# A 16-head masked attention feeding two expert layers on one Trainium2 core: a bank evacuation and four weight-load issues moved along ScalarE's queue

## The chip, the cores and the metric

The kernel runs on one core of a Trainium2 chip. The metric is device time in microseconds (us) of one launch, the median of several runs. The kernel before takes 790.23 us (median of 3 runs, 789.36 to 791.34).

## The reference, cut to what matters

Three layers follow each other. The change lies in the first; the weights that it loads earlier belong to the second.

```python
# attention: B=2, H=8, S=768, D=64 -> 16 heads, 16 clusters per head
q_assign = argmax(normalised q . normalised centroids); k_assign likewise
scores = where(q_assign == k_assign, q @ k.T / sqrt(D), -1e9)
attn = exp(scores - max) ; attn = attn / (sum(attn) + 1e-9)
x = attn @ v                                   # heads side by side: 1536 x 512
# layer 2
h = x @ w_in ; g = s * relu(h)**2 + b ; x = g @ w_out      # d_ff = 2048, float64 weights
# layer 3: each of the 1536 tokens goes to one of 8 experts
out[token] = gate * (relu(x @ w1[e]) @ w2[e])
```

## The kernel before, in words

**Attention is a written-out order.** `attention` (L94) gives every piece of work a time on one line: head `j` owns the 12 slots from `12*j`, and a piece with offset `t` in the table `TIMES` (L31) stands at `12*j + t`. All pieces are sorted by this number (L375) and `Order.pin` (L59) keeps each engine's instructions in that order. So a number in the table sets only the order in each engine's queue; when an instruction runs is decided by its waits. Below, "frame k" is the stretch of head `k`'s twelve slots, and pieces of heads before and after fall into it.

In a frame TensorE (PE) does, slot by slot, one product `M` for a later head (L223; VectorE reduces it to a row maximum, L224) and one pair of products `S` for this head (L247, L248; ScalarE turns it into `pt` with Exp, L249). `S` has two tile names for the two halves of a row of keys, `s0` and `s1`, one PSUM bank each, so the pair of slot 5 writes the bank that the Exp of slot 3 reads. `V` (L264) multiplies `pt` with the values into the single bank `pv`: six groups per head, done two by two at slots 5.45, 9.45 and 1.45 of the next frame. `pv_out` (L272) is two ScalarE instructions that read this bank, `vm` (L276) and `xu` (L277); the next head's first `V`, at slot 5.45, overwrites it. `trans` (L157) turns `k` and `q` of a head three frames ahead: three PE transposes into the single bank `t` (L162) and one ScalarE copy out of it (`kb` or `qb`, L168). The two for `k` stand at slots 11.4 and 0.4, the two for `q` at 2.4 and 3.4; of each two the second waits for the copy of the first. `mrow` (L232, slot 8.5) writes the row maxima of the next head as one row of `qa`: a ScalarE copy `mrs` (L237) and a DMA on SyncE's queue (L238, `qa<-mrs`). The next head's first `S`, at slot 0 of the next frame, reads that row.

**Weights of layer 2.** `conv_steps` (L416) turns one 128-row piece of the float64 weights to float32 in nine steps, and the last step calls `load_f64` (L523) for the piece three further on: two DMAs of 512 KB, `w_in` (L525) and `w_out` (L526), into the pool `raw`. For the pieces 0 to 3 these are issued from ScalarE's queue, at the time `36*f + 16 + CONV[8]`. With `CONV[8]` = 31.2 this is slot 11.2 of frames 3, 6, 9 and 12. Three first loads (`FETCH`, slot 5.3 of frames 0, 1 and 2) are issued from the same queue.

```python
37   CONV = (3.2, 5.2, 7.2, 11.2, 15.2, 19.2, 23.2, 27.2, 31.2)
373  for i, f in enumerate((pv_out, sums, norm_a, norm_b, norm_c)):
374      at(o + ENDS.get(j, T["norm"])[i], f, j)
407  for n, t in enumerate(CONV):
408      out.append((36 * f + 16 + t if f < NWA - 1 else 176.2 + n, ...
276  nc.scalar.activation(out=vm, in_=pp[:, HS:HS + 1], func=AF.Copy, scale=GUARD / S)
277  nc.scalar.activation(out=xu, in_=pp[:, 0:HS], func=AF.Identity, bias=vm[:, 0:1])
```

Of the kernel before, what the change touches and what calls it, by code (L numbers as in the profile page):

```python
# [28 lines left out]
MASK = float(2 ** 33)  # L29
GUARD = 1e-9  # L30
TIMES = dict(load=-49, loadv=-18, split=(-42, -40), trans=(-36.6, -35.6, -33.6, -32.6), sims=-30.53, simv=(-26.5, -26.5, -26.5, -22.52, -22.52, -22.51),  # L31
             M=-17.4, mneg=-5.7, mrow=-3.5, V=(5.45, 5.45, 9.45, 9.45, 13.45, 13.45), presum=3.0, norm=(14.5, 25.47, 29.5, 29.5, 29.5))
ENDS = {14: (14.5, 21.47, 22.4, 23.4, 24.4), 15: (14.5, 14.6, 14.7, 14.8, 14.9)}
WARM = -26
HEAT = ((-41, 7), (-30.5, 6), (-22, 6))
SETUP, FETCH = 6.3, (5.3, 17.3, 29.3)
CONV = (3.2, 5.2, 7.2, 11.2, 15.2, 19.2, 23.2, 27.2, 31.2)
F, DM, TC = 2048, 512, 512
NF, KD, NTT = F // P, DM // P, TC // P
E, F2 = 8, 1024  # L40
# [53 lines left out]
def attention(ax, tc, cst, q, k, v, cen, xt, hooks, embed):  # L94
# [124 lines left out]

    def M(j, r, c):  # L220
        i = j % NSET
        pp = ps([P, HS], "M", f"M{c}" if j else ("M0", "M1", "s0", "s1", "s2")[(2 * r + c) % 5])
        nc.tensor.matmul(pp, qa[i][0:80, r * P:(r + 1) * P], ka[i][0:80, c * HS:(c + 1) * HS])  # L223
        nc.vector.tensor_reduce(out=mxt[j % 2][:, r, c:c + 1], in_=pp, axis=AX.X, op=ALU.max)  # L224
# [112 lines left out]
    def at(t, f, *a):  # L337
        ops.append((t, len(ops), f, a))
# [9 lines left out]
    for j in range(NH):  # L348
# [12 lines left out]
        for r in range(NR):  # L361
            for c in range(2):
                at(o + T["M"] + 2 * r + c, M, j, r, c)
                if j == 0:
                    at(o + T["M"] + 2 * r + c, cst.heat, 2, "pv")
        at(o + T["mneg"], mneg, j)
# [14 lines left out]
class Moe:  # L381
# [11 lines left out]
    def hooks(self, ms, mb):  # L393
# [12 lines left out]
        for f in range(NWA):  # L406
            for n, t in enumerate(CONV):
                out.append((36 * f + 16 + t if f < NWA - 1 else 176.2 + n, lambda f=f: next(self.steps(f), None)))
# [51 lines left out]
    def ps(self, shape, name, tag):  # L460
        return self.cst.ps(shape, name, dict(a="pv", b="sm", y0="t", y1="s0", y2="s1", y3="s2").get(tag, tag))
# [124 lines left out]
    def moe1(self, xt):  # L586
# [4 lines left out]
        for c in range(self.chunks):  # L591
# [4 lines left out]
            def up(f):  # L596
# [4 lines left out]
                if final:  # L601
                    self.load_expert(f + 1)
                    if f in PRE0:
                        z = PRE0.index(f)
                        with self.after(*tail):
                            self.pre0[z] = self.half(self.wraw[0, z], 0, nc.gpsimd, False)
                hp = self.ps([P, TC], "hp", f"M{f % 2}")
                self.up_mm(hp, *wu, lambda k: x[k // 2][:, k % 2], lambda k: x[2 + k // 2][:, k % 2])
# [446 lines left out]
    def block(self, y, args, w, pre, hooks, wd=None, g0=None):  # L1055
# [7 lines left out]
        def up(f):  # L1063
            with ExitStack() as behind:
# [5 lines left out]
                if f not in wd:  # L1070
                    wd[f] = self.half(w[f], 1, nc.vector)
            hp = self.ps([P, T], "hp", f"M{f % 2}")
            if xl is None:
# [121 lines left out]
```

## Time and profile before

| | |
|---|---|
| median of 3 runs | 790.23 us (789.36 to 791.34) |
| the profiled execution's own time | 785.38 us |
| its span, first to last instruction | 783.5 us, mean granted TensorE clock 0.987 |
| PE busy over the span | 747.7 us (95%) |
| DVE (VectorE), ACT (ScalarE), POOL (GpSimd) busy | 518.4, 423.3, 352.1 us |

The profile is of one execution. Times in rows are us from the span's start. An engine's name with a q is its instruction queue (ACTq, SPq): those rows are DMA issues, during which the queue takes nothing else. PEld is the weight load of a product. A row's last part in brackets is the time that the engine sat idle before it, and what the profile takes for the end of that wait. Products overlap on PE, so the step from one start to the next says what one costs, not its own duration.

### The profile page before, as it was taken

Reading aid. Unit: us, or ns where it says so; the run is one execution under the profiler, and the core shown is the slowest. Engines: PE = TensorE matmul, PEld = TensorE weight load, DVE = VectorE, ACT = ScalarE, POOL = GpSimd, SP = SyncE. Lnnn points to the kernel's source line nnn. Section 1 sums busy time; section 2 is a strip of 40 time slices with the busy share of each in tenths; the row PEclk is TensorE's granted clock in tenths of the full one; section 3 lists DMA queues with packets and bytes.
Section 4 is the critical chain, followed back from the end, with each engine's and each line's share of the span. In section 5 each row is a group of like instructions: output and inputs, shape, how many; then the busy total and the mean of one; then the engine's idle time right before and its main releaser. Section 6 shows DMA issues by size and latency. Waiting matters only on the chain. (4 is left out here: it accounts for less than half of the span.)

```text
span 783.5 us, 12256 instructions
## 1 busy us (share of the span) xinstructions
PE 747.7 (95%) x4193; PEld 564.0 (72%) x4193; DVE 518.4 (66%) x1100; ACT 423.3 (54%) x843; POOL 352.1 (45%) x282
## 2 busy tenths in 40 slices
PE   7799999999999899999999999999999999999993
PEld 3465555565555468888787887877879998988983
DVE  5768989797997889984354442557567365755750
ACT  5266555655554576555445564454557365755650
POOL 3166776676685565445333544467132302230001
PEclk9899999999999999999999999999999999999997
DMA  5145443434322225511000042265235555865600
GB/s 154 42 129 176 107 124 81 140 87 135 79 64 80 69 61 171 161 55 54 1 1 1 1 161 82 81 215 167 80 117 177 184 192 179 250 215 195 220 17 24
DMA packets 75678, 88.72 MB, mean 113 GB/s; under 512 B 7526, under 2 KB 58630, under 8 KB 75345
## 3 DMA queue, kind: packets, MB, share of 16 engines
q1 hardware_dynamic: 66688, 66.52, 28.1%
q0 software_dynamic: 4208, 13.90, 5.5%
q10 hardware_dynamic: 4704, 7.34, 2.8%
q8 instruction: 40, 0.66, 0.3%
q14 instruction: 38, 0.30, 0.1%
HBM read 70.57 MB, written 7.34 MB: 99 GB/s over the span
## 5 line engine op out<-in xcount | busy, mean ns | idle before, releaser
L534 POOL TENSOR_TENSOR wl<-w,wh 128x512 fp32r<-128x512 f32 x96 | 123.0, 1306 | 128.8 <-ACT wh L532 126.1
L249 ACT ACTIVATE pt<-S 128x384 f32<-128x384 f32 x192 | 91.8, 489 | 101.1 <-PE S L248 98.8
L224 DVE TENSOR_REDUCE mx<-M 128x1 f32<-128x384 f32 x192 | 101.9, 552 | 37.1 <-PE M L223 34.6
L260 POOL TENSOR_TENSOR acc<-acc,pt 128x768 f32<-128x768 f32 x61 | 106.0, 1737 | 5.7 <-ACT pt L249 3.3
L555 PE MATMUL hp<-x,wh 128*128 128x512 f32 x384 | 105.1, 395 | 0.3 <-ACT wh L532 0.3
L555 PE MATMUL hp<-x,spare 128*128 128x256 f32 x732 | 96.0, 284 | 2.0 <-PEq L987 1.7
L555 PEld LDWEIGHTS hp<-x,spare 128*128 128x128 f32 x732 | 92.6, 190 | 6.9 <-issue 4.1
L563 PE MATMUL y<-wd,gg 128*128 128x512 f32 x360 | 93.2, 394 | 0.0
L611 DVE SCALAR_TENSOR_TENSOR hp<-hp,sb,t 128x512 f32<-128x512 f32 x48 | 36.4, 758 | 74.6 <-ACT t L610 74.6
L223 PE MATMUL M<-ka,qa 80*128 80x384 f32 x192 | 79.0, 412 | 4.2 <-DVE mx L224 3.1
L555 PEld LDWEIGHTS hp<-x,wh 128*128 128x128 f32 x384 | 70.6, 188 | 15.1 <-ACT wh L532 0.9
L563 PE MATMUL y<-wh,gh 128*128 128x512 f32 x192 | 74.9, 390 | 0.0
L563 PE MATMUL y<-wl,gh 128*128 128x512 f32 x192 | 74.7, 389 | 0.0
L247 PE MATMUL S<-qa,ka 97*128 97x384 f32 x192 | 71.0, 370 | 2.1 <-ACT pt L249 1.4
L268 PE MATMUL pv<-pt,vn 128*64 128x385 f32 x384 | 72.8, 500 | 0.0
L548 DVE TENSOR_TENSOR wd<-w,wd 128x512 fp32r<-128x512 f32 x64 | 43.3, 686 | 44.1 <-ACT wd L547 43.3
L563 PEld LDWEIGHTS y<-wd,gg 128*128 128x128 f32 x360 | 63.8, 189 | 9.9
L1036 POOL DMA_INDIRECT row<-rows,idx x24 | 27.9, 1163 | 88.0 <-PE tp L1048 49.1
L248 PE MATMUL S<-qb,kb 128*128 128x384 f32 x192 | 65.5, 341 | 0.0
L610 ACT ACTIVATE t<-hp 128x512 f32<-128x512 f32 x48 | 28.7, 598 | 67.6 <-PE hp L555 67.5
L223 PEld LDWEIGHTS M<-ka,qa 80*128 80x128 f32 x192 | 36.9, 192 | 38.2 <-DVE su L296 8.1
L532 ACT ACTIVATE wh<-w 128x1024 fp32r<-128x1024 f32 x48 | 50.4, 1055 | 17.7 <-PE y L563 12.9
(275 smaller groups left out, 1352.2 us busy)
## 6 DMA issues: line engine op xcount, KB each, us to landing
w<-in_moe_w_dram SPq DMA_DIRECT2D x128, 256.0 KB
raw<-in_moe_w_in_dram SPq DMA_DIRECT2D x9, 512.0 KB
raw<-in_moe_w_out_dram SPq DMA_DIRECT2D x9, 512.0 KB
raw<-in_moe_w_in_dram ACTq DMA_DIRECT2D x7, 512.0 KB
raw<-in_moe_w_out_dram ACTq DMA_DIRECT2D x7, 512.0 KB
qn<-in_q_dram SPq DMA_DIRECT2D x16, 192.0 KB
kn<-in_k_dram SPq DMA_DIRECT2D x16, 192.0 KB
vn<-in_v_dram SPq DMA_DIRECT2D x16, 192.0 KB
```

Source lines behind the costliest of these rows:

```text
L223: nc.tensor.matmul(pp, qa[i][0:80, r * P:(r + 1) * P], ka[i][0:80, c * HS:(c + 1) * HS])
L224: nc.vector.tensor_reduce(out=mxt[j % 2][:, r, c:c + 1], in_=pp, axis=AX.X, op=ALU.max)
L247: nc.tensor.matmul(pp, ka[i][0:97, t * P:(t + 1) * P], qa[i][0:97, w], start=True, stop=False)
L248: nc.tensor.matmul(pp, kb[i][:, t * P:(t + 1) * P], qb[i][:, w], start=False, stop=True)
L249: exps.setdefault((j, t), []).append(nc.scalar.activation(out=p[:, c, 0:HS], in_=pp, func=AF.Exp, scale=0.125).ins)
L260: eng.tensor_tensor(out=acc[j][-1], in0=acc[j][-1], in1=p[:, :, 0:HS], op=ALU.add)
L268: together(tc, [lambda c=c: nc.tensor.matmul(pv_t[j][c * 64:c * 64 + 64, :], io_t["v", j][:, t, :], p[:, c, :], start=t == 0, stop=t == NR ...
L532: nc.scalar.activation(out=wh, in_=w, func=AF.Copy)
L534: eng.tensor_tensor(out=wl[:, a], in0=w[:, a], in1=wh[:, a].bitcast(F32), op=ALU.subtract)
L548: eng.tensor_tensor(out=t[:, 1], in0=w[:, a], in1=t[:, 0].bitcast(F32), op=ALU.subtract)
L555: self.nc.tensor.matmul(hp, a[:, k * P:(k + 1) * P], b(k), start=n == 0, stop=n == 3 * KD - 1)
L563: self.nc.tensor.matmul(y[i], (gl if n == 2 else gh)[:, s], wl if n == 1 else wh, start=first and n == 0, stop=last and n == 2)
```

## The change

Two numbers of the tables change. `pv_out` of heads 0 to 13 moves from slot 14.5 to 15.45 of its head, that is from slot 2.5 to 3.45 of the next frame. The issue of the four pairs of weight loads moves from slot 11.2 to 9.48 of frames 3, 6, 9 and 12.

```diff
 TIMES = dict(load=-49, ...
-             M=-17.4, ..., presum=3.0, norm=(14.5, 25.47, 29.5, 29.5, 29.5))
+             M=-17.4, ..., presum=3.0, norm=(15.45, 25.47, 29.5, 29.5, 29.5))
 ENDS = {14: (14.5, 21.47, 22.4, 23.4, 24.4), 15: (14.5, 14.6, 14.7, 14.8, 14.9)}
...
-CONV = (3.2, 5.2, 7.2, 11.2, 15.2, 19.2, 23.2, 27.2, 31.2)
+CONV = (3.2, 5.2, 7.2, 11.2, 15.2, 19.2, 23.2, 27.2, 29.48)
```

Only ScalarE's queue is reordered. In frame 10, around slot 3, the queue reads as follows (`qb` are the copies out of the query transposes, `pt` the Exps):

```order
 L249 ACTIVATE pt_129<-S 128x384
 L168 ACTIVATE qb_117<-tp 128x384
-L276 ACTIVATE vm<-pv 128x1
-L277 ACTIVATE xu<-pv,vm 128x384
 L249 ACTIVATE pt_129<-S 128x384
 L168 ACTIVATE qb_117<-tp 128x384
+L276 ACTIVATE vm<-pv 128x1
+L277 ACTIVATE xu<-pv,vm 128x384
 L249 ACTIVATE pt_130<-S 128x384 x2
```

The evacuation of `pv` goes behind one Exp (slot 3) and the second query copy. Frames 1 to 12 look like this; in frames 13 and 14, where no head is left to transpose, it goes behind the Exp alone.

On PE nothing moves, but the waits do. In frame 10 at slot 5.45 the program before has:

```order
L247 MATMUL S<-qa_110,ka_114 128x384 [waits Activation_49]
L248 MATMUL S<-qb_118,kb_122 128x384
L268 MATMUL pv<-pt_128,vn 64x385 x2
L268 MATMUL pv<-pt_129,vn 64x385 x2
L178 MATMUL si<-qb_117,cc 32x384 [waits Activation_49]
```

and the changed one:

```order
L247 MATMUL S<-qa_110,ka_114 128x384 [waits Activation_49]
L248 MATMUL S<-qb_118,kb_122 128x384
L268 MATMUL pv<-pt_128,vn 64x385 [waits Activation_49]
L268 MATMUL pv<-pt_128,vn 64x385
L268 MATMUL pv<-pt_129,vn 64x385 x2
```

The first `V` product of the head now has a wait for ScalarE of its own: for `xu`.

In frame 9, around the weight loads, ScalarE's queue reads:

```order
 L237 ACTIVATE mrs<-mr 6x128
 L249 ACTIVATE pt_126<-S 128x384
-L249 ACTIVATE pt_127<-S 128x384 x2
 L525 DMA raw<-in_moe_w_in_dram 128x4x256
 L526 DMA raw<-in_moe_w_out_dram 128x1024
+L249 ACTIVATE pt_127<-S 128x384 x2
 L168 ACTIVATE kb_121<-tp 128x384
```

The two issues go ahead of two Exps, and no longer stand right before the copy `kb`. They now follow the copy `mrs` with one Exp between.

## Rows read from the trace of the kernel before

**Rows 1.** Busy time by engine, 60 to 260 us (PE, PEld, DVE, ACT, POOL; clock, DMA).

```profile
60.00:260.00 200.00, 193.33 (x1088) 116.33 (x1085) 170.99 (x357) 113.53 (x276) 141.31 (x90) 1.00 0.37 105
```

**Rows 2.** Timeline, frame 10, ACT (start, duration, engine, line, operation).

```profile
194.35 0.49 ACT L168 ACTIVATE qb<-tp 128x384 fp32r<-128x384 f32 x1
...
194.93 0.58 ACT L277 ACTIVATE xu<-pv,vm 128x384 f32<-128x384 f32 x1
```

**Rows 3.** Timeline, frame 10, PE.

```profile
194.89 0.45 PE L162 MATMUL tp<-identr,qs 128*128 128x128 f32 x3 [0.21 <-ACT vm L276]
...
195.95 0.44 PE L247 MATMUL S<-qa,ka 97*128 97x384 f32 x1
...
196.50 0.54 PE L268 MATMUL pv<-pt,vn 128*64 128x385 f32 x2
```

**Rows 4.** Timeline, frame 13, PE.

```profile
239.27 0.34 PE L248 MATMUL S<-qb,kb 128*128 128x384 f32 x1
...
240.18 0.34 PE L223 MATMUL M<-ka,qa 80*128 80x384 f32 x1
240.78 0.45 PE L247 MATMUL S<-qa,ka 97*128 97x384 f32 x1 [0.25 <-ACT pt L249]
...
241.33 0.54 PE L268 MATMUL pv<-pt,vn 128*64 128x385 f32 x2
```

**Rows 5.** Timeline, end of frame 9 and start of 10, PE.

```profile
188.71 0.45 PE L223 MATMUL M<-ka,qa 80*128 80x384 f32 x1
188.99 0.34 PE L247 MATMUL S<-qa,ka 97*128 97x384 f32 x1
...
190.00 0.45 PE L162 MATMUL tp<-identr,ks 128*128 128x128 f32 x3 [0.48 <-ACT kb L168]
...
190.98 0.54 PE L268 MATMUL pv<-pt,vn 128*64 128x385 f32 x2
```

**Rows 6.** Timeline, end of frame 8 (no load issued there), PE.

```profile
173.55 0.45 PE L223 MATMUL M<-ka,qa 80*128 80x384 f32 x1
...
175.12 0.54 PE L268 MATMUL pv<-pt,vn 128*64 128x385 f32 x2
```

**Rows 7.** Timeline, end of frame 9, ACT and its queue.

```profile
186.20 0.46 ACT L249 ACTIVATE pt<-S 128x384 f32<-128x384 f32 x1
187.93 0.97 ACT L249 ACTIVATE pt<-S 128x384 f32<-128x384 f32 x2 [1.27 <-PE S L248]
188.47 0.39 ACTq L525 DMA_DIRECT2D raw<-in_moe_w_in_dram  x1
```

**Rows 8.** Timeline, issues of the row of maxima: frame 9, frame 14.

```profile
186.32 0.77 SPq L238 DMA_DIRECT2D qa<-mrs  x1
...
259.22 0.73 SPq L238 DMA_DIRECT2D qa<-mrs  x1
```

**Rows 9.** Timeline, start of frame 15, PE.

```profile
261.13 0.41 PE L247 MATMUL S<-qa,ka 97*128 97x384 f32 x1 [0.43 <-DMA qa<-mrs]
```

**Rows 10.** Timeline, a transfer on SP's queue with no weight load near it (frame 9).

```profile
180.76 0.53 SPq L170 DMA_DIRECT2D qa<-qb  x1
```

**Rows 11.** DMA queues, 181.90 to 183.10 us (packets, MB, share of 16 engines; q1 is SP's).

```profile
q1 hardware_dynamic: 80, 0.20, 74.3%
```

**Rows 12.** Timeline, ACT's and SP's queue, frame 0.

```profile
42.71 0.43 ACTq L525 DMA_DIRECT2D raw<-in_moe_w_in_dram  x1
...
43.06 0.54 SPq L170 DMA_DIRECT2D qa<-qb  x1
```

**Rows 13.** DMA queues, 44.21 to 45.80 us (q10, ACT's, is the only one listed).

```profile
q10 hardware_dynamic: 353, 0.36, 82.0%
```

**Rows 14.** Timeline, SP's and ACT's queue, frame 1.

```profile
57.87 0.58 SPq L123 DMA_DIRECT2D vn<-in_v_dram  x1
...
57.94 0.40 ACTq L525 DMA_DIRECT2D raw<-in_moe_w_in_dram  x1
```

**Rows 15.** DMA queues, 59.72 to 60.24 us (again the only one listed).

```profile
q10 hardware_dynamic: 97, 0.10, 81.3%
```

More of the change, by code (lines that the diff above doesn't have):

```diff
@@ L31 @@
 TIMES = dict(load=-49, loadv=-18, split=(-42, -40), trans=(-36.6, -35.6, -33.6, -32.6), sims=-30.53, simv=(-26.5, -26.5, -26.5, -22.52, -22.52, -22.51),
-             M=-17.4, mneg=-5.7, mrow=-3.5, V=(5.45, 5.45, 9.45, 9.45, 13.45, 13.45), presum=3.0, norm=(14.5, 25.47, 29.5, 29.5, 29.5))
+             M=-17.4, mneg=-5.7, mrow=-3.5, V=(5.45, 5.45, 9.45, 9.45, 13.45, 13.45), presum=3.0, norm=(15.45, 25.47, 29.5, 29.5, 29.5))
 ENDS = {14: (14.5, 21.47, 22.4, 23.4, 24.4), 15: (14.5, 14.6, 14.7, 14.8, 14.9)}
```

## The prediction

> **What bounds the kernel now.** I began with the busy time by engine for the stretch in which all the moved pieces lie, 60 to 260 us [rows 1]. PE is busy 193.3 of 200 us; ScalarE, whose queue is the only one reordered, 113.5. So ScalarE's work is worth nothing in itself. The change counts only where PE stands and waits for a ScalarE instruction, or for a DMA. There I read the timelines of PE and of ScalarE side by side: one frame for the evacuation of `pv` [rows 2, 3], the first of the two frames without transposes [rows 4], and the end of a frame with weight loads against one without [rows 5 to 7]. The reader is to look at the starts on PE: where the step from one product to the next is longer than elsewhere, the bracket or the ScalarE row that ends just before says who was late.
>
> Three late places touch the change. In frame 10 the `S` at 195.95 takes 0.44 us where others take 0.34 [rows 3, 5]: its bank was freed by the Exp of slot 3, which queued behind `vm` and `xu`, so its weights were loaded late. I read 0.10 us lost per frame. In frame 13 the same wait is longer [rows 4]. At the end of frame 9 PE stands 0.48 us for the copy `kb`, and the copy stands behind two load issues [rows 5, 7]. The wait of the second query transposes (0.21 us, put down to `vm`) is in truth for the copy of the first, which ends at 194.35 + 0.49 = 194.84, 0.05 before the start at 194.89 [rows 2, 3]; that copy does not move, so this wait stays.
>
> **The evacuation in frames 1 to 12.** No instruction is added or removed. The Exp of slot 3 comes free of `vm` and `xu`, so `S` of slot 5 no longer loads its weights late: 0.10 us gained. But `xu` is now the last thing before `V` at slot 5.45, which overwrites its bank and has a wait for it. When is `xu` done? The second query transposes end at 194.89 + 0.45 = 195.34 [rows 3] and do not move. The copy starts some 0.05 later, at 195.39 (the 0.05 of above). From a copy's start to the start of `xu` behind it is 194.93 - 194.35 = 0.58, and `xu` takes 0.58 [rows 2]: it ends at 196.55. With another 0.05 to wake PE, `V` starts at 196.60; it starts at 196.50 now [rows 3]. So the 0.10 gained is spent waiting, and 0.10 more with it. Behind `V` on PE stand the similarity products and all the rest of the frame, and all of it waits. Over 12 frames: **+1.2**. I hold the step good to 0.05 a frame; if `xu` were no bound, the 0.10 would remain a gain, -1.2. The two Exps behind `xu` run later too; the `V` products cover that, since nothing reads those results before the next group.
>
> **The evacuation in frames 13 and 14.** Here no transposes hold it up. The Exp of slot 3 can start when its `S` is done, 239.27 + 0.34 + 0.05 = 239.66 [rows 4]. `xu` starts 0.58 later and ends at 240.82, `V` starts at 240.87. PE itself could be there at 240.91 at most (from `M` at 240.18, 0.28 to `S` as in [rows 5], 0.45 to `V` without late weights). It starts at 241.33 now: 0.42 to 0.46 gained, in two frames: **-0.9**. The end to the other side is nothing, if the wait merely moves to `xu`.
>
> **The loads out of the way of `kb`.** In frame 9 it is 190.98 - 188.71 = 2.27 us from `M` to `V` [rows 5]; in frame 8, with the same work and no load, 175.12 - 173.55 = 1.57 [rows 6]. That is 0.70 us a frame. Frames 3 and 6 show the same pattern; in frame 12 there is no `kb` left. **-2.1** for three frames, between that and nothing. In their new place the two issues start right behind the Exp of slot 9, and ScalarE stands idle for 1.27 us after it [rows 7]; two issues of 0.39 to 0.43 us [rows 7, 12, 14] fit in. If that cover were missing, 0.4 us would come back on the Exps of slots 10 and 11.
>
> **What the loads now run into.** The issue moves past the row of maxima. In frame 9 the first load would be issued at about 186.25 (0.05 behind the start of an Exp, as at present), and `qa<-mrs` is issued on SP's queue at 186.32 [rows 7, 8]. The first `S` of the next head needs that row. Where it waited for it, in frame 15, it started 261.13 - 259.22 = 1.91 us after the issue [rows 8, 9]. In frame 9 it could thus start at 188.23 and does at 188.99 [rows 5]: 0.76 us of slack. Does a load of 512 KB eat that? No row of before shows this pair. Without loads near it a transfer on SP's queue has all its packets within 181.90 to 183.10, from 1.14 us after its issue at 180.76 [rows 10, 11]. The like transfer issued at 43.06, 0.35 us after a load, has not one packet until 45.80; only the load's queue moves [rows 12, 13]. That is 45.80 - 44.20 = 1.6 us late. The transfer `vn` issued at 57.87, 0.07 us before a load, has none before 60.24 [rows 14, 15], against 59.01 by the 1.14: 1.2 late. So the delay lies between 0 and 1.6; a gain is excluded, since the row's issue itself does not move. I take 1.2, the row nearest in issue time. `S` then waits 1.2 - 0.76 = 0.44 and loses 0.10 on late weights: 0.54, in three frames **+1.6** (taken alike in all three; in frame 12 the gap is longer by what `kb` no longer uses, so I count nothing). By the 1.6 it would be 0.94 each, +2.8. The other transfers that now meet the loads, `qn` and `kn`, are read a frame later.
>
> The Trainium skill, "DMA: Bandwidth & Descriptors", section "Queues, rings and completion order", says that each engine takes turns between the queues that have work, a packet at a time. By that rule a row of a few packets would hardly be held up at all; the rows speak against it, with a whole stretch in which one queue alone moves.
>
> **The sum.** +1.2 - 0.9 - 2.1 + 1.6 = **-0.2 us**. It is made against the profiled execution (785.38 us, of which 1.9 us lie outside its span). The median shown is 790.23, 4.85 above it; I take the difference over: **790.0 us**. With the delay of the maxima at its ends, 0 and 1.6 us, the sum is -1.8 and +1.0: 788.4 to 791.2. A measurement here can tell a change of about 0.3%, 2.4 us; the forecast is thus "no change".
>
> **The rivals.**
> *The row of maxima is not held up.* It is small, and if its packets slip in between the load's, the stall of 1.6 goes. Time 790.23 - 1.8 = 788.4, still within 0.3%. For it speaks the rule above and that its issue is within 0.1 us of the load's; against it the two late transfers [rows 12 to 15]. 0.23.
> *`xu` does not bind.* If the evacuation ends before PE is ready for `V`, the 0.10 stays in twelve frames: -1.2 - 0.9 - 2.1, with the stall 1.6 or none, -2.6 to -4.2: 786.0 to 787.6, faster. It needs the transposes to end 0.2 us earlier than [rows 3] shows, so I give it 0.10.
> *Slower: the row waits for the whole first load.* In [rows 13] the load moves 0.36 MB in 1.59 us, so 0.52 MB take some 2.3 us. If the row's packets stand behind all of it, `S` stalls 2.3 - 0.76 + 0.10 = 1.64 in three frames: +4.9 instead of +1.6, sum +3.1, **793.3**. It decides from a delay of about 2.1 us on (2.4 + 1.8 = 4.2 over three frames, 1.4 each). For it: the transfer of frame 0 was late by most of such a load. Against: neither transfer was late by more than 1.6. 0.10.
> *The loads do not move.* Their issue also waits for the buffers' last reader; if that ended late, the issue would hold ScalarE and the place would gain nothing: +1.2 - 0.9 = +0.3, 790.5. The reader is the VectorE step at slot 7.2, ahead of this `V` group, so 0.09.
>
> **How the numbers follow.** The forecast as summed has 0.48. It, the first rival and the last lie within 0.3%: 0.80 the same. Faster takes the second rival: 0.10. Slower the third: 0.10. The range leaves out those two and reaches to the cases within: the first rival's 788.4 and the bound at 791.2, with half a microsecond below and one above for the 0.05 a frame that I cannot read off: 787.9 to 792.2.
>
> **What would show it.** Right: in frame 10 `V` starts some 1.7 us after the second query transposes (1.61 now), its idle time ended by `xu`; `S` of slot 5 takes 0.34; in frame 13 `V` follows `M` of slot 5 by about 0.7 (1.15 now); the transposes for `k` in frames 3, 6 and 9 no longer wait for `kb`; and `S` at slot 0 there waits for `qa<-mrs` by about 0.4. Wrong: no wait for `qa<-mrs` (first rival), one over 1.3 us (third), or a `V` that follows `S` of slot 5 by 0.45 (second).

## The result, and the profile after

The changed kernel takes **803.57 us** (median of 6 runs, 795.41 to 805.82), the kernel before beside it 790.47 us (6 runs, 789.36 to 791.34). The ratio is **1.0149, 95% interval 1.0101 to 1.0196**: slower, well outside the range. Its runs lie five times as far apart as those of before, and their mean granted TensorE clock goes with it: 0.981 in the two shortest, 0.971 to 0.976 in the four longest.

The profiled execution is the shortest of the six, 795.41 us. Three sections of it, read from the first `V` and the last `xu` of attention and from layer 3's first `ge` (L874), beside three of the runs below:

| us | before | after | change again (e9) | with filler (e6) | loads on SyncE (e3) |
|---|---|---|---|---|---|
| first `V` to the end of the last `xu` | 233.95 | 238.87 | 248.07 | 240.66 | 232.17 |
| from there to layer 3's first `ge` | 283.04 | 283.08 | 283.01 | 283.13 | 283.10 |
| from there to the end | 223.92 | 228.85 | 227.74 | 223.87 | 227.83 |

All that the change does lies in the first line. Ahead of the first `V` the traces take 41.4 to 47.0 us, in no order of the kernels (42.60 before, 42.73 after, 44.94 in e9). The last line differs by 4 to 5 us too, but not by kernel: the experiments were made in three sets, the first and the third on one chip and the second on another. All four traces of the second set have 223.9 to 224.2 there, all eight of the others 227.4 to 228.0. The medians of before in the three sets, 790.2, 786.59 and 789.55, go the same way. So the shown profile of before has the short end, and the medians beside it the long one; that would be most of the 4.85 us that the prediction carried over.

Where attention lost time, the waits say. Total, times and longest wait, PE and its weight loads, 60 to 260 us, first before:

```profile
PE tp L162 <- ACT kb L168: 2.1, 7, 0.5
```

and after:

```profile
PEld pv L268 <- ACT xu L277: 5.6, 13, 0.5
PE S L247 <- DMA qa<-mrs: 5.3, 4, 2.2
...
PE tp L162 <- ACT kb L168: 0.2, 1, 0.2
```

The wait for `kb` has gone, as forecast. In its place `S` waits four times for the row of maxima, 5.3 us in sum; before it waited for that row nowhere in this stretch. The wait for `xu` is one of the weight loads of `V`, which run ahead of the products; what it costs PE is read in the frames. The windows row that answers to [rows 1]:

```profile
60.00:260.00 200.00, 188.62 (x1069) 114.89 (x1063) 167.80 (x350) 110.36 (x269) 137.51 (x87) 1.00 0.38 104
```

PE lost 4.7 of 200 us of busy time, at full clock. Frame 10 on PE and on ScalarE, answering to [rows 3] and [rows 2]:

```profile
199.66 0.45 PE L162 MATMUL tp<-identr,qs 128*128 128x128 f32 x3 [0.21 <-ACT qb L168]
...
200.72 0.34 PE L247 MATMUL S<-qa,ka 97*128 97x384 f32 x1
...
201.36 1.51 PE L268 MATMUL pv<-pt,vn 128*64 128x385 f32 x8
```

```profile
200.14 0.49 ACT L168 ACTIVATE qb<-tp 128x384 fp32r<-128x384 f32 x1 [0.15 <-PE tp L162]
...
200.72 0.58 ACT L277 ACTIVATE xu<-pv,vm 128x384 f32<-128x384 f32 x1
```

`V` starts 1.70 us after the transposes (1.61 before), 0.06 after `xu` ends at 201.30; `S` takes 0.34 instead of 0.44. Frame 13, answering to [rows 4]:

```profile
245.81 0.34 PE L223 MATMUL M<-ka,qa 80*128 80x384 f32 x1
...
246.50 1.19 PE L268 MATMUL pv<-pt,vn 128*64 128x385 f32 x6
...
249.47 0.44 PE L223 MATMUL M<-ka,qa 80*128 80x384 f32 x1 [0.20 <-DVE mx L224]
```

From `M` to `V` it is 0.69 us, 1.15 before. But three microseconds on PE stands for VectorE's row maximum `mx`, a wait that before does not have there.

Now the loads. The issues on ScalarE's and SyncE's queues at the end of frames 6, 9 and 12, answering to [rows 7] and [rows 8]:

```profile
141.77 0.39 ACTq L525 DMA_DIRECT2D raw<-in_moe_w_in_dram  x1
...
142.06 0.76 SPq L238 DMA_DIRECT2D qa<-mrs  x1
142.25 0.46 ACTq L526 DMA_DIRECT2D raw<-in_moe_w_out_dram  x1
...
190.55 1.72 ACTq L526 DMA_DIRECT2D raw<-in_moe_w_out_dram  x1
190.63 0.77 SPq L238 DMA_DIRECT2D qa<-mrs  x1
...
236.93 0.75 SPq L238 DMA_DIRECT2D qa<-mrs  x1
237.40 1.32 ACTq L526 DMA_DIRECT2D raw<-in_moe_w_out_dram  x1
```

PE at the start of the frames behind them (3, 6, 9 and 12), answering to [rows 5] and [rows 9]:

```profile
99.11 0.41 PE L247 MATMUL S<-qa,ka 97*128 97x384 f32 x1 [1.85 <-DMA qa<-mrs]
...
147.38 0.41 PE L247 MATMUL S<-qa,ka 97*128 97x384 f32 x1 [2.20 <-DMA qa<-mrs]
...
194.41 0.41 PE L247 MATMUL S<-qa,ka 97*128 97x384 f32 x1 [0.94 <-DMA qa<-mrs]
...
240.78 0.41 PE L247 MATMUL S<-qa,ka 97*128 97x384 f32 x1 [0.32 <-DMA qa<-mrs]
```

And the queues from 143.50 to 146.00 us, in frame 6 (packets, MB, share of 16 engines):

```profile
q10 hardware_dynamic: 556, 0.82, 97.9%
```

The row was issued at 142.06. With no load near it, its six packets begin 1.35 to 1.46 us after the issue (eleven rows of this trace); here that would be 143.45. Instead ScalarE's queue alone moves 0.82 of the 1.05 MB of the two loads, and the row's first packet comes at 146.09, 2.6 us late. In frames 3, 6, 9 and 12 the row's first packet is 2.6, 2.6, 0.8 and 1.4 us late, its last 2.9, 3.2, 1.7 and 1.7 us. `S` needs the whole row: in all four it starts 0.64 or 0.65 us behind the start of the last packet.

Frame lengths sum it up (one first `V` to the next): an ordinary frame 15.28 to 15.31 us (15.16 to 15.19 before); frames 3, 6 and 9 together 51.40 (47.63).

### The profile page after: what moved, and what is told of

Same layout as the page of the kernel before. It is cut to its first block, busy times and chain, and to the rows that moved or that the text cites. A ratio compares the mean times of both kernels' runs of the same rounds, so it can differ in the third digit from the quotient of the medians.

```text
span 793.5 us, 12254 instructions
## 1 busy us (share of the span) xinstructions
PE 750.6 (95%) x4191; PEld 567.8 (72%) x4193; DVE 518.4 (65%) x1100; ACT 423.1 (53%) x843; POOL 352.6 (44%) x282
```

## The experiments

Three sets, each on one chip with its own runs of before: 790.2 us (e1 to e4), 786.59 us (e5 to e8), 789.55 us (e9 to e12, on the chip of the first set). Theory: the row of maxima is late behind the loads, `S` stalls, and in most executions the stall is followed by half clock. Main rivals: the later evacuation of `pv`, or traffic as such. In the diffs, `-` is the kernel before unless said otherwise.

**e1: the evacuation alone.**

```diff
-norm=(14.5, 25.47, 29.5, 29.5, 29.5)
+norm=(15.45, 25.47, 29.5, 29.5, 29.5)
```

> Only the evacuation of pv moves (slot 15.45); the weight loads stay at slot 11.2. If the row of maxima behind the loads makes the whole loss (row theory), this kernel is within 1.5 us of the one before: V waits for xu, some 0.1 us in each of twelve frames, and frames 13 and 14 give back 0.4 us each; no wait for qa<-mrs in frames 3 to 13, and no fall of the granted clock between 60 and 260 us. If the wait for xu makes the loss (bank theory), it is slower by 5 us or more.

Measured 791.34 us, ratio 1.0010 (0.9996 to 1.0024). Ordinary frames 15.27 to 15.29, the two steps from frame 12 to 13 and from 13 to 14 are 14.00 and 12.98 (14.47 and 13.12 before). From frame 1 to the end of attention the frames add up to +0.4 us, where the sum gave +0.3; this leaves out the step from frame 0 to frame 1, which takes 15.22 to 15.84 us in these traces (15.84 here, but 15.59 in e10, which has no late evacuation). The loss isn't there.

**e2: the loads alone.**

```diff
-CONV = (..., 27.2, 31.2)
+CONV = (..., 27.2, 29.48)
```

> Only the loads move (slot 9.48); pv is evacuated at 14.5 as before. Row theory: slower than before by nearly as much as the whole change (5 us in attention, more where the clock falls, 8 to 14 us in the median), with waits of S for qa<-mrs of 1 to 2.3 us at the start of frames 4, 7, 10 and 13. Bank theory: faster than before by up to 2.1 us.

Measured 801.03 us, 1.0120 (1.0068 to 1.0171). PE's waits, 60 to 260 us:

```profile
PE S L247 <- DMA qa<-mrs: 7.3, 4, 2.3
```

The move of the loads alone makes the loss. Frames 3, 6, 9 and 12 take 20.10, 20.77, 18.96 and 18.89 us, more than the waits explain: behind each of the four stalls the granted clock is 0.5 for 3.4 to 6.8 us.

**e3: the loads at the same place, but from SyncE's queue, behind the row.**

```diff
-CONV = (..., 27.2, 31.2)
+CONV = (..., 27.2, 29.48)
-self.loaded[f + 3] = self.load_f64(f + 3, nc.scalar if f < NWA - 1 else nc.sync)
+self.loaded[f + 3] = self.load_f64(f + 3, nc.sync)
```

> The loads at slot 9.48 again, but issued from SyncE's queue, right behind the row of maxima instead of beside it; pv as before. Row theory: the row is through before the loads start, no wait for qa<-mrs there, and the copies kb are free of the issues: 1.5 to 2.5 us faster than before. If it is not the order of row and loads but loads this early that harm (for instance by holding up the transfers behind them), it stays 5 us or more slower.

Measured 787.72 us, 0.9962 (0.9943 to 0.9982): faster than before. SyncE's queue at the end of frame 9:

```profile
185.89 0.76 SPq L238 DMA_DIRECT2D qa<-mrs  x1
186.70 0.43 SPq L525 DMA_DIRECT2D raw<-in_moe_w_in_dram  x1
...
187.23 0.44 SPq L526 DMA_DIRECT2D raw<-in_moe_w_out_dram  x1
```

The same bytes, issued 0.8 us behind the row's issue, and no row of the four is late by more than 0.02 us; `S` does not wait. Whether it is the queue or the 0.8 us that does it this run can't tell: from ScalarE's queue the loads were tried 0.2 us behind the row's issue (e4) and 1.7 us (e10), not between. Frames 3, 6 and 9 take 15.19, 15.19 and 15.39: 0.71, 0.68 and 0.48 less than before. That is the gain by `kb`, without its price.

**e4: the loads as in the change, the row one place earlier.**

```diff
-mrow=-3.5
+mrow=-4.52
-CONV = (..., 27.2, 31.2)
+CONV = (..., 27.2, 29.48)
```

> The loads at slot 9.48 from ScalarE's queue as in the change, but the row of maxima goes a slot earlier (7.48), so that its issue is about 1 us ahead of the loads instead of within 0.1 us; pv as before. Row theory: the wait for qa<-mrs is gone and the kernel is within 1.5 us of before or up to 2 us faster (PE may wait some 0.2 us a frame for the maxima). If lying behind the loads is not what delays the row, it stays 5 us or more slower.

Measured 790.95 us, 1.0015 (0.9996 to 1.0034). The place in the order brought the row only 0.17 us ahead of the first load. Queues in frame 6, and PE's waits:

```profile
140.27 0.77 SPq L238 DMA_DIRECT2D qa<-mrs  x1
...
140.44 0.39 ACTq L525 DMA_DIRECT2D raw<-in_moe_w_in_dram  x1
140.92 0.46 ACTq L526 DMA_DIRECT2D raw<-in_moe_w_out_dram  x1
```

```profile
PE S L247 <- DMA qa<-mrs: 1.7, 3, 0.6
```

The row is still late, by 0.7 to 1.6 us, though its issue *starts* first. Half a microsecond between row and loads took the stall from 7.3 us (e2) to 1.7 and nearly all of the loss with it.

**e7 and e8: one load at a time.** Only `w_in` (512 packets of 1 KB), or only `w_out` (128 of 4 KB), at the new place; the other stays at 31.2.

```diff
-CONV = (..., 27.2, 31.2)
+CONV = (..., 27.2, 29.48, 31.2); HALVES = (0, 1)
...
+for n, a in enumerate(HALVES):
+    if n:
+        yield
...
```

(in e8 `HALVES = (1, 0)`)

> Of each pair of loads only that of w_in is issued at slot 9.48 (ScalarE's queue), that of w_out at 11.2 as before; pv as before. If the row of maxima waits for the load just ahead of it, w_in with its 512 packets of 1 KB, it is as late as in e2 (packets some 4 us after the issue, waits of about 2 us), and the time is that of e2, 797 to 803 us. If it waits for both loads or for the second, the waits shrink to under 1 us.

> The reverse: w_out (as many bytes, in 128 packets of 4 KB) at slot 9.48 and w_in at 11.2; pv as before. If the delay of the row goes by the bytes ahead of it, this equals e7. If it goes by the number of pieces ahead of it, the row is late by a quarter of that, under 0.8 us, S does not wait for it, and the kernel is within 2 us of before.

Measured 792.88 us, 1.0093 (1.0068 to 1.0118), for `w_in` first; 788.12 us, 1.0024 (1.0004 to 1.0045), for `w_out` first. The stalls in the two traces, 60 to 260 us, e7 and then e8:

```profile
PE S L247 <- DMA qa<-mrs: 1.2, 3, 0.4
```

```profile
PE S L247 <- DMA qa<-mrs: 1.4, 3, 0.6
```

With one load beside it the row is 0.7 to 1.6 us late, of whichever piece size; with both, up to 2.6. So it is the loads ahead that count, not the number of their pieces. Why e7's runs were longer than e8's isn't settled: its profiled execution, 787.62 us, is the shortest of four, and the other three (791.66 to 795.89) left no trace.

**The order of the issues' ends.** e4 and frames 9 and 12 of the change made me put the ends of the issues (start plus duration) side by side. In the 28 cases of the traces of after, e2, e4 and e6 to e9:

| the row's issue ended | cases | row's first packet late by, us |
|---|---|---|
| after both loads' issues | 10 | 2.20 to 2.63 |
| after that of the first, before that of the second | 10 | 0.74 to 1.62 |
| after that of a single load (e7, e8) | 8 | 0.74 to 1.58 |

Frame 6 of after shows the first kind: the row's issue ends at 142.06 + 0.76 = 142.82, `w_out`'s at 142.25 + 0.46 = 142.71. Frames 9 and 12 show the second: `w_out`'s issue took 1.72 and 1.32 us there and ended at 192.27 and 238.72, after the row's, although in frame 9 it started first. The packets themselves agree. In the ten cases of the first line all of `w_in`'s 512 pieces (510 in one) and 63 to 108 of `w_out`'s 128 started before the row's first packet; in the ten of the second, 132 to 458 of `w_in`'s and at most two of `w_out`'s. That the row stood behind one load or two is thus shown; that the end of the issue decides it is a sorting of traces, since no run moved an issue's end alone.

**e6: the change, with filler products on PE ahead of the stalling `S`** (against the changed kernel; nine bf16 products into scratch at the start of frames 4, 7, 10 and 13).

```diff
-        at(o + T["sims"], sims_mm, j)
+        at(o + T["sims"], sims_mm, j); [at(o - 0.2, cst.heat, 9, "s1") for _ in range(j in (4, 7, 10, 13))]
```

> The whole change, and nine idle products on PE (128 x 512, bf16, their result unused) ahead of the first S of frames 4, 7, 10 and 13, in the place of the wait. The row of maxima comes as late as in the change. If what the change loses beyond its waits is the granted clock falling after PE stood still, the clock stays up between 60 and 260 us and the loss is that of the waits alone: 5 to 7 us over before, 796 to 797 us, and not 803. If the clock has no part in it, the time is that of the change or longer.

Measured 792.80 us, 1.0078 (1.0061 to 1.0095). PE in frame 6, and its windows row:

```profile
145.60 0.45 PE L223 MATMUL M<-ka,qa 80*128 80x384 f32 x1
145.89 2.12 PE L1133 MATMUL heat<-work 128*128 128x512 bf16 x8
147.66 0.53 PE L247 MATMUL S<-qa,ka 97*128 97x384 f32 x1
```

```profile
60.00:260.00 200.00, 193.65 (x1092) 116.65 (x1093) 165.43 (x346) 108.33 (x263) 136.40 (x86) 1.00 0.38 105
```

The stall is still there, filled (2.06 us from `M` to `S`). The four runs lie within 0.7 us, the clock is full from 60 to 260 us, and about half of the loss has gone. The intervals of e6 and of the change (1.0101 to 1.0196, and 1.0156 to 1.0209 in e9) do not meet: the clock is worth about as much as all the rest. The change without filler was not run on the chip of e6, so each ratio is to before on its own chip.

**e9: the change once more.** The changed kernel as it is.

> The change itself once more, for a second trace. Theory (row of maxima late by 1.4 to 2.6 us behind both loads, then a stretch at half clock in some executions): S waits for qa<-mrs in frames 3, 6, 9 and 12, in sum 4 to 8 us; the frames with loads are 16.4 to 18.5 us long and the ordinary ones 15.28 to 15.31; about 1.0 to 1.7% slower than before; where a frame is longer than its wait explains, the granted clock is 0.5 for some microseconds behind the wait. Rival (the loss is elsewhere, such as at the start of layer 3): the frames with loads sum to no more than 3 us above the other kernel's and the rest of the loss lies behind 300 us.

Measured 804.82 us, 1.0182 (1.0156 to 1.0209). PE in frame 6, and windows around it (columns as in [rows 1]):

```profile
149.00 0.44 PE L223 MATMUL M<-ka,qa 80*128 80x384 f32 x1
151.45 0.66 PE L247 MATMUL S<-qa,ka 97*128 97x384 f32 x1 [2.00 <-DMA qa<-mrs]
```

```profile
140.00:149.00 9.00, 8.72 (x52) 5.03 (x50) 8.29 (x20) 5.08 (x14) 5.56 (x5) 1.00 0.45 114
149.00:151.30 2.30, 0.44 (x1) 0.18 (x1) 0.96 (x2) 0.55 (x2) 2.22 (x2) 1.00 1.03 394
151.30:158.20 6.90, 6.75 (x21) 3.44 (x22) 1.77 (x4) 1.36 (x3) 2.70 (x2) 0.51 0.25 66
158.20:165.00 6.80, 6.45 (x41) 4.11 (x40) 5.01 (x12) 3.59 (x10) 1.83 (x1) 1.00 0.15 35
...
202.50:209.40 6.90, 6.43 (x21) 3.12 (x21) 1.77 (x4) 1.36 (x3) 2.63 (x2) 0.51 0.25 65
```

The second row is the stall; in the third PE is busy throughout and has 21 products where the fourth, as long, has 41. The granted clock of 0.51 is the lower of the two levels, 1.2 of 2.4 GHz. The same follows the stalls at the end of frame 3 (3.4 us of half clock) and of frame 9 (the last row). Frames 3, 6 and 9 take 60.48 us together, 9.1 more than in the profile of after. There the stalls were as long (1.85 and 2.20 us) and no half clock followed.

**e10: the loads alone, one slot later** (`CONV[8]` = 30.48, ScalarE's queue).

```diff
-CONV = (..., 27.2, 31.2)
+CONV = (..., 27.2, 30.48)
```

> The loads alone, on ScalarE's queue, one slot later (slot 10.48, behind one more Exp), so that the row of maxima is issued some 1.3 to 1.7 us ahead of them. Theory (the row is late only if the loads are issued together with it): no wait for qa<-mrs, no half clock between 60 and 260 us, and a time within 0.3% of before, or up to 2 us faster by what kb no longer waits. Rival (any load on ScalarE's queue near the end of the frame holds the row up): S still waits for qa<-mrs by over 0.5 us in three frames and the time is 0.5 to 1.2% above before.

Measured 789.35 us, 0.9997 (0.9984 to 1.0010). End of frame 9:

```profile
190.98 0.77 SPq L238 DMA_DIRECT2D qa<-mrs  x1
...
192.68 0.39 ACTq L525 DMA_DIRECT2D raw<-in_moe_w_in_dram  x1
...
194.59 0.45 PE L162 MATMUL tp<-identr,ks 128*128 128x128 f32 x3 [0.42 <-ACT kb L168]
```

1.7 us ahead of the loads the row is on time, `S` does not wait, and the loss is gone, on the same queue with the same bytes. `kb` is late again (frames of 15.80 us), so nothing is gained either.

**e11 and e12: the better version.** e11 is e3 again; e12 adds the late evacuation in heads 12 and 13 alone. **e5** is the same kernel as e12, in the second set.

```diff
-ENDS = {14: (14.5, ...
+ENDS = {12: (15.45, 25.47, 29.5, 29.5, 29.5), 13: (15.45, 25.47, 29.5, 29.5, 29.5), 14: (14.5, ...
```

> The loads at slot 9.48 from SyncE's queue (e3), and the evacuation of pv at 15.45 in frames 13 and 14 alone, where no transpose stands between. Row and bank theory together: e3's gain of 2.5 us and 0.4 us from each of the two frames, 787 us or 3.3 us under the kernel before. If a late evacuation gives nothing even there, it equals e3.

> The four pairs of loads at the place of the change but from SyncE's queue, behind the row, once more beside the change on one chip. Theory: no wait for qa<-mrs, 0.7, 0.7 and 0.5 us gained in frames 3, 6 and 9: 2 to 3 us faster than before, 0.25 to 0.4%. Rival (its first result was a chip's): no difference from before.

> The loads from SyncE's queue and the late evacuation of pv in heads 12 and 13 alone (frames 13 and 14), beside the same without the late evacuation. Theory (frames 13 and 14 gain 0.47 and 0.1, ordinary frames lose 0.11 only where the evacuation is late): 0.5 to 0.7 us faster than the run with the loads alone, 2.5 to 3.2 us faster than before. Rival (the gain of frames 13 and 14 is given back before the end of attention): the same as the run with the loads alone.

| | median, us | ratio to before |
|---|---|---|
| e5 | 783.98 | 0.9968 (0.9955 to 0.9980) |
| e11 | 788.12 | 0.9979 (0.9961 to 0.9997) |
| e12 | 787.10 | 0.9966 (0.9951 to 0.9981) |

Both beat the kernel before. e12 is 1.0 us below e11, which the intervals don't separate; their frames do: the steps from frame 12 to 14 take 27.03 us in e12, 27.60 in e11.

## Why the prediction was wrong

**The evacuation in frames 1 to 12 (+1.2): right.** Ordinary frames are 0.10 to 0.12 us longer, in the change and in e1 alone, by the mechanism given: `V` follows `xu`.

**Frames 13 and 14 (-0.9): half right.** Both `V` come 0.46 us earlier behind their `M`, but the frames gain 0.47 and 0.14 in e1: -0.6. What is late next in frame 13 was not asked: the row maximum on VectorE, 3 us on.

**`kb` (-2.1): right.** e3 shows it by itself: 0.71 + 0.68 + 0.48 = 1.9. The issues also fit into ScalarE's idle time in frames 3 and 6, as said; in frames 9 and 12 that of `w_out` took 1.72 and 1.32 us, which no row of before has.

**The row of maxima (+1.6): here it failed**, at "the delay lies between 0 and 1.6" and "I take 1.2, the row nearest in issue time". From `M` to the stalling `S` PE lost 2.01, 2.36, 1.11 and 0.48 us in frames 3, 6, 9 and 12, beyond the 0.28 of an undisturbed step: 6.0 in sum. Three things in the step were wrong.

*The loads ahead of the row.* The two transfers of [rows 12] and [rows 14] were compared by when their issues began. ScalarE's queue in the kernel before, timeline, at those two places:

```profile
43.19 0.61 ACTq L526 DMA_DIRECT2D raw<-in_moe_w_out_dram  x1
...
58.37 0.58 ACTq L526 DMA_DIRECT2D raw<-in_moe_w_out_dram  x1
```

Those second loads' issues ended at 43.80 and 58.95; the transfers' own at 43.06 + 0.54 = 43.60 and 57.87 + 0.58 = 58.45. Both stood behind one load, and their 1.6 and 1.2 us are what a row behind one load shows in the table above. In frames 3 and 6 of the changed kernel the row of maxima, whose issue takes 0.76 us, ended its own behind both.

*When the loads are issued.* The prediction put the first load 0.07 us ahead of the row's issue, 0.05 behind the start of an Exp. It came 0.28, 0.28 and 0.56 us ahead in frames 3, 6 and 9 (0.01 in frame 12). In frame 9 ScalarE's queue issued it before the Exp that stands ahead of it in the order had begun, and before `mrs`, whose end the row's issue waits for:

```profile
190.07 0.39 ACTq L525 DMA_DIRECT2D raw<-in_moe_w_in_dram  x1
190.36 0.25 ACT L237 ACTIVATE mrs<-mr 6x128 f32<-6x128 f32 x1
190.51 0.46 ACT L249 ACTIVATE pt<-S 128x384 f32<-128x384 f32 x1
```

At the predicted times the issue of `w_out` would have ended about 0.1 us after the row's (186.25 + 0.94 = 187.19, with the 0.94 of frame 6 of after, against 186.32 + 0.77 = 187.09). So the rows of before, read by the ends of issues, would still have given a row behind one load.

*The first packet for the whole row.* Delay and wait were both read as if the first packet counted. Frame 9 shows that it does not: the first packet was 0.8 us late, hardly more than the slack of 0.76, and yet 1.11 us were lost, since the last was 1.7 us late. The slack, too, is that of frame 9 alone: in frames 3 and 6 of before the `S` starts 2.95 and 2.96 us after the row's issue, by the prediction's 1.91 a slack of 1.04 and 1.05.

With what the terms measured the sum closes: +1.4 (twelve times 0.12) - 0.6 - 1.9 + 6.0 = +4.9, and attention is 4.92 us longer in the profile of after.

**What the sum had no term for: the clock.** In e9 frames 3, 6 and 9 are 12.85 us longer than before. The waits for the row there are 6.4 us (1.98 + 2.00 + 2.40); with the 1.9 gained by `kb` and the 0.4 lost to `xu` that leaves 12.85 - 6.4 + 1.9 - 0.4 = 8.0 us for the 17.3 us at a clock of 0.51, more than the stalls themselves. e6 fills the stalls and loses no clock. That the four longest runs of the change spent their time above 795.41 us in the same way is likely by their mean clocks (0.971 to 0.976), not shown; the run of 799.02 us has the mean clock of the shortest.

**The rivals.** "Not held up" did not happen: one queue had 97.9% of the engines' time for 2.5 us while the row waited. The prediction leaned on the Trainium skill, "DMA: Bandwidth & Descriptors", section "Queues, rings and completion order" (turns between queues, a packet at a time), and read its packet as one of the trace's pieces. There it is a batch of descriptors, 9 to 17 as a rule and 64 at most; by an estimate with these figures, and the pieces spread evenly over 16 engines, `w_in` has 512 / 16 = 32 on each. The row waited for all of them and for most of `w_out`'s in the ten cases of the table's first line, more than the page's usual batch; a batch of 64 would cover it, so the rule itself is not refuted here. The slower rival had the right kind (a whole load ahead of the row, a wait over 1.3 us) at 0.10, but one load too few and no clock: 793.3. `xu` does bind, and the loads did move.

## What to carry to other kernels

A small transfer that an engine waits for should not be issued together with large loads on another queue: here 3 KB behind two loads of 512 KB came 2.2 to 2.6 us late. Issued 0.2 us ahead of the loads it was still 0.7 to 1.6 us late; 1.7 us ahead, or with the loads 0.8 us behind it on its own queue, it was on time. When a trace is searched for a price of such a meeting, count the loads whose issue has ended ahead of the transfer's, and take the transfer's last packet, not its first. And a stall of some 2 us on a busy TensorE is not priced by its length alone: look in several executions at what the granted clock does behind it.

## What the runs showed of the hardware that was not expected

- In the 20 cases with both loads a DMA's place among the queues goes with the end of its issue, not the start: the row is 0.7 to 1.6 us late where the second load's issue ended after the row's, 2.2 to 2.6 us where it ended before (no exception; issues that start in the same order are in both groups).
- ScalarE's queue can issue a DMA before the instructions ahead of it in the order have begun: by 0.44 us in frame 9 of after (190.07 against 190.51).
- Pieces of 1 KB and of 4 KB hold a row up alike (0.74 to 1.44 us in e7, 0.98 to 1.58 in e8).
- Half clock for 3.4 to 6.9 us behind all seven stalls of 1.25 to 2.40 us in the traces of e2 and e9, and behind none in that of after, where three were 0.94 to 2.20 us long. What decides between the two stays open.
- The last section of the kernel, untouched, takes 224 us on the chip of the second set and 227.4 to 228.0 on that of the other two. In the profile of after, PE waits there once for 3.2 us behind two late `ge`, and the granted clock is 0.5 for 6.8 us from 582.9 on; the eight traces of the first and third set have 3.4 us of half clock some 20 us into this section, those of the second none there:

```profile
575.92 0.28 ACT L874 ACTIVATE ge<-hpe 128x128 f32<-128x128 f32 x1 [3.05 <-PE tp L1048]
578.16 0.28 ACT L874 ACTIVATE ge<-hpe 128x128 f32<-128x128 f32 x1 [1.96 <-PE ye L878]
```

```profile
583.89 0.47 PE L733 MATMUL si<-vals,ohr 128*128 128x24 bf16 x12 [3.18 <-DVE vals L781]
```

The same product starts after an idle time of 0.23 us in the profile of before. What makes `ge` late there was not tried.
